# Projection inputs of blocks 1 to 3: normalised in place on ScalarE, turned in 32x32 blocks by VectorE

## The chip, the cores and the metric

The kernel runs on one core of a Trainium2 chip. The metric is the device time of one execution in microseconds; the number given for a kernel is the median of several runs. The engines named below are TensorE (PE, with its weight loads PEld), VectorE (DVE), ScalarE (ACT), GpSimd (POOL) and SyncE (SP, which only issues transfers here). Each works through its own queue of instructions in order, and semaphores hold an instruction until what it needs is there.

## What is computed

```python
xn = layernorm(x)                       # x: 2048 x 512, mean and variance over the 512
q, k, v = split(xn @ wqkv)              # 32 heads of 16
s = softmax(q k^T / 4) v  @ wo          # full attention over 2048 keys
f = (silu(xn @ w_gate) * (xn @ w_up)) @ w_down      # 512 -> 1792 -> 512
out = x + s * silu(f)
```

All inputs and the output are float32. Only the step from `x` to the transposed, normalised `xn` that the projections read is touched by the change.

## The kernel before

The 2048 rows are cut into four blocks of 512 rows, and each block into four tiles of 128 rows. The kernel has two stages. The first, some 148 us, makes the projections: for each block in turn, twelve output tiles, eight of them for features of q and k (`feature_tile`) and four for values (`value_tile`). In block 0 the value tiles come first (slots n = 0 to 3) and the feature tiles after them (n = 4 to 11); in blocks 1 to 3 the feature tiles are n = 0 to 7 and the value tiles n = 8 to 11. The second stage, all the rest of the time, is the attention, with the feed-forward network woven into it (`run`, `fill`, `ffn`).

An output tile (`project`, L648) is twelve matmuls on one PSUM bank. Operands are split into a rounded part and the rest (`hi`, `lo`), so for each of the four 128-wide chunks c of the inner dimension there are three matmuls in this order: hi with the weights' hi, lo with the weights' hi, hi with the weights' lo. Four PSUM banks (`pps`) take turns. After a feature tile ScalarE squares it (L701) and rounds it into `parts` (L702), VectorE subtracts to get the rest (L703), and SyncE stores both. After a value tile ScalarE copies it into `vt` (L719).

The projections need the normalised rows with features on the partitions, as `xt[b % 2]`, a pair of tiles hi and lo; two pairs take turns by block. While block b is projected, block b+1 is made ready in pieces between its slots, and the order is written out by hand in the loop at L745 to L827; each engine runs its share in that program order:

- `load_x` (L546): four transfers of 128 rows into `xin`, which is the tile `facc` (shown as such in the profile). Issued at n = 2 of block 0 and n = 1 of blocks 1 and 2.
- `stats` (L608) on VectorE for one tile at each of n = 2 to 5, and `rates` (L613) at n = 5: a chain of small VectorE operations around one square root on ScalarE (L616), which gives `rs`, one over the standard deviation.
- `norm` (L625) on VectorE for one tile at each of n = 6 to 9: (x - mean) * rs, into `xn`.
- `turn_x` (L641) at n = 8, 9 and twice at n = 10: four TensorE transposes of 128x128 into a bank of `acc` (L631), then ScalarE rounds it into hi (L636) and VectorE subtracts into lo (L639). After the last tile GpSimd's queue issues the two stores of the pair to `xt_d` (L645), from where the feed-forward network reads it hundreds of microseconds later.

Other work on the same queues in this stage: `split_w` (L568) rounds a tile of weights on ScalarE (L574) and subtracts on GpSimd (L575). In block 0 it is called at slot n for the weights of the tile n + 2, up to n = 9. `copy_fx` (L727, L732) puts one of sixteen pieces of block 0's `xt` into `fx` on ScalarE; it is called after the tile in each slot from n = 3 of block 0 to n = 6 of block 1. `flush` (L740) sums the squares of the tiles made so far with small matmuls (L663, in `squares`) and takes their peak; it stands at n = 0 of block 1 for block 0, and behind tile n = 8 in blocks 1 to 3. The sums need ScalarE's squares of all the eight feature tiles.

## Time and profile before

| | us |
|---|---|
| median of 3 runs | 1405.37 (1405.2 to 1405.68) |
| the profiled execution | 1405.18 |
| its span in the trace | 1403.4 |
| block 0 to 3 of the projections start at about | 6, 46, 83, 119 |
| PE busy over the span | 1395.8 |
| ACT busy over the span | 1082.7 |
| DVE busy over the span | 753.5 |
| POOL busy over the span | 90.6 |

A timeline row gives the start, the length, the engine, the line of the kernel, the operation, what it writes and reads, how many instructions are merged in the row, and in brackets the idle time before it with what ended it. The length of an instruction is from its start to its end; the next one on the same engine often starts somewhat before that end, so the cost of a row in a queue is the distance between starts. On TensorE this is marked: the lengths of matmuls overlap, and only the distance from start to start tells what one costs.

### The profile page before, as it was taken

The numbers are of one execution on the slowest core, as the hardware profiler recorded it, in microseconds if no ns is written. First come the engines' busy times: TensorE is split into PE (matmuls) and PEld (weight loads), VectorE is DVE, ScalarE is ACT, GpSimd is POOL, SyncE is SP. The second block draws the span as 40 slices with busy tenths as digits, with TensorE's granted clock in tenths as the row PEclk, the third lists the DMA queues.
The fourth block names the chain that finished last, engine by engine and source line by source line (L and its number), as shares of the span: only waits on it lengthen the run. The fifth ranks groups of instructions, "written<-read, shape, count | busy, mean of one in ns | idle before, by whom it ended". The sixth has DMA issues, their size and how long they took to land.

```text
span 1403.4 us, 27734 instructions
## 1 busy us (share of the span) xinstructions
PE 1395.8 (99%) x11227; PEld 847.1 (60%) x11227; DVE 753.5 (54%) x1291; ACT 1082.7 (77%) x1235; POOL 90.6 (6%) x104
## 2 busy tenths in 40 slices
PE   9999999999999999999999999999999999999998
PEld 7777756556555655565556556655655565565554
DVE  5544455345645553555456645654565446556655
ACT  6733587778788877887887788778877887888885
POOL 4200200000000000000000000000000000000333
PEclk9999999999999999999999999999999999999999
DMA  6768651033544521144524303256224113224333
GB/s 219 263 248 247 181 128 43 13 103 88 122 102 103 125 50 35 47 118 107 131 64 104 101 13 73 73 143 145 65 73 109 37 46 73 66 89 162 102 99 113
DMA packets 126956, 148.17 MB, mean 106 GB/s; under 512 B 12524, under 2 KB 79340, under 8 KB 126052
## 3 DMA queue, kind: packets, MB, share of 16 engines
q1 hardware_dynamic: 121620, 125.79, 34.2%
q0 software_dynamic: 4912, 20.12, 3.9%
q8 instruction: 91, 1.49, 0.4%
q14 instruction: 45, 0.37, 0.1%
q10 hardware_dynamic: 288, 0.39, 0.1%
HBM read 106.68 MB, written 39.58 MB: 104 GB/s over the span
## 4 chain that ended last, share of the span: by engine, by line
PE 88%; ACT 0%; DVE 0%; issue 0%; DVEq 0%; ACTq 0%
PE acc L406 32%; PE bankx L186 24%; PE score L888 17%; PE banky L186 12%; PE acc L888 3%; PE acc L1015 0%; PE banky L1015 0%; ACT pr L961 0%; ACT pr L894 0%; PE score L1015 0%; DVE y L1022 0%; DVE fx L280 0%; DVE part L300 0%; DVE y L191 0%; DVE pr L947 0%
## 5 line engine op out<-in xcount | busy, mean ns | idle before, releaser
L894 ACT ACTIVATE pr<-score 128x1024 f32<-128x1024 f32 x856 | 810.6, 1032 | 229.3 <-PE score L888 227.8
L406 PE MATMUL acc<-pr,vst 128*17 128x512 f32 x4096 | 461.9, 593 | 0.0
L888 PE MATMUL score<-qst,kst 50*128 50x512 f32 x1712 | 392.0, 413 | 0.0
L186 PE MATMUL bankx<-fx,guh 64*128 64x512 f32 x896 | 333.4, 393 | 0.1
L186 PE MATMUL banky<-fx,guh 64*128 64x512 f32 x896 | 324.5, 392 | 0.0
L406 PEld LDWEIGHTS acc<-pr,vst 128*17 128x17 f32 x4096 | 108.8, 97 | 286.4 <-issue 262.6
L888 PEld LDWEIGHTS score<-qst,kst 50*128 50x128 f32 x1712 | 176.0, 184 | 147.7 <-issue 67.2
L947 DVE COPY pr<-acc 128x512 f32<-128x512 f32 x168 | 116.2, 691 | 192.5 <-PE acc L888 187.0
L186 PE MATMUL bankx<-wd,hh 64*128 64x512 f32 x672 | 200.2, 392 | 0.0
L186 PE MATMUL banky<-wd,hh 64*128 64x512 f32 x672 | 197.8, 393 | 0.0
L186 PEld LDWEIGHTS bankx<-fx,guh 64*128 64x128 f32 x896 | 166.4, 186 | 18.0 <-issue 0.9
L186 PE MATMUL bankx<-fx,gul 64*128 64x512 f32 x448 | 175.4, 391 | 0.0
L186 PE MATMUL banky<-fx,gul 64*128 64x512 f32 x448 | 175.4, 391 | 0.0
L961 ACT ACTIVATE pr<-pr 128x1024 f32<-128x1024 f32 x168 | 172.5, 1079 | 0.0
L186 PEld LDWEIGHTS banky<-fx,guh 64*128 64x128 f32 x896 | 166.3, 186 | 6.1
L953 DVE COPY pr<-acc 128x512 f32<-128x512 f32 x168 | 116.2, 692 | 73.8 <-PE acc L888 60.3
L888 PE MATMUL acc<-qst,kst 50*128 50x512 f32 x336 | 135.4, 403 | 0.1
L239 DVE SCALAR_TENSOR_TENSOR ga<-th,bankx 128x512 f32<-128x512 f32 x56 | 38.5, 688 | 178.2 <-ACT th L238 178.2
L186 PEld LDWEIGHTS bankx<-wd,hh 64*128 64x128 f32 x672 | 124.9, 186 | 12.4
L186 PEld LDWEIGHTS banky<-wd,hh 64*128 64x128 f32 x672 | 124.4, 186 | 3.6
L186 PEld LDWEIGHTS bankx<-fx,gul 64*128 64x128 f32 x448 | 83.7, 187 | 10.3
L186 PEld LDWEIGHTS banky<-fx,gul 64*128 64x128 f32 x448 | 83.5, 186 | 3.6
(168 smaller groups left out, 1308.7 us busy)
## 6 DMA issues: line engine op xcount, KB each, us to landing
gur<-in_B_w_gate_dram SPq DMA_DIRECT2D x56, 256.0 KB
gur<-in_B_w_up_dram SPq DMA_DIRECT2D x56, 256.0 KB
wdr<-in_B_w_down_dram SPq DMA_DIRECT2D x56, 256.0 KB
kst<-k_d SPq DMA_DIRECT2D x192, 64.0 KB
qst<-q_d SPq DMA_DIRECT2D x192, 64.0 KB
fx<-xt_d SPq DMA_DIRECT2D x24, 512.0 KB
q_d<-parts SPq DMA_DIRECT2D x16, 512.0 KB
k_d<-parts SPq DMA_DIRECT2D x16, 512.0 KB
```

Of the source, the lines that this page charges most:

```text
L186: mm(banks[i], lhs[halves[i]], rhs[halves[i]], start=start, stop=stop)
L239: dve.scalar_tensor_tensor(ga, th, 1.0, bankx, op0=ALU.add, op1=ALU.mult)
L406: mm(acc[0][h * 32:h * 32 + DH + 1], v[:, kt % CT, h * (DH + 1):(h + 1) * (DH + 1)], probs[kt, h // 2][:, h % 2], start=kt == 0, stop=kt = ...
L888: mm(bank, k[r, j, kc * P:(kc + 1) * P], qst[u % 2][r, j], start=True, stop=True)
L894: act(pr, score[slot], AF.Exp, scale=0.25)
L947: dve.tensor_copy(probs[kt, j][:, 0], spare_bank)
L953: dve.tensor_copy(probs[kt, j][:, 1], spare_bank)
L961: act(probs[kt, j], probs[kt, j], AF.Exp, scale=0.25)
```

## The change

For blocks 1 to 3 the rows are normalised in place by ScalarE: `norms` first makes `off = -mean * rs` for the four tiles in one small VectorE operation and then runs four activations `xin * rs + off` with both as per-partition columns. They stand where `rates` stands, at n = 5 of block 0 and, since the statistics move one slot earlier, at n = 4 of blocks 1 and 2; there `load_x` moves from n = 1 to n = 0 as well. VectorE's `norm` goes.

The transposes on TensorE go, too. VectorE turns the rows in 32x32 blocks: `turn_quarter` takes 32 partitions of `xin` (quadrant g) and writes the blocks of one feature quarter to 32 partitions (quadrant q) of a new tile `xw`, sixteen instructions for a block of rows, each of 512 elements on 32 partitions. They stand ahead of the tile of a slot: in block 0 at n = 6 to 11 in numbers of 2, 3, 3, 2, 3, 3, in blocks 1 and 2 at n = 5 to 11 in numbers of 2, 2, 2, 3, 2, 2, 3. The rounding into hi and the subtraction into lo, which were done by row tiles at n = 8 to 10, are done by chunks c in `split_block` behind the tile and the other work of n = 11, and the two stores to `xt_d` behind them. Block 0 keeps the old way.

```diff
+TURNS = [[(max(0, min(16, s * (n - f) // d)), max(0, min(16, s * (n + 1 - f) // d))) for n in range(12)]
+         for f, s, d in ((6, 8, 3), (5, 16, 7))]
...
+        xw = pc.tile([P, DT, TB], F32, name="xw")
...
+        off = pc.tile([P, NT], F32, name="off")
...
             split_x(b, t, turn(t), between)
-            if t == NT - 1 and b:
-                for j in range(2):
-                    pool.dma_start(xt_d[b, j], xt[b % 2][j].bitcast(F32))
+
+        def norms():
+            dve.scalar_tensor_tensor(off, mv[:, :, 0], -1.0, rs, op0=ALU.mult, op1=ALU.mult)
+            for t in range(NT):
+                act(xin[:, t], xin[:, t], AF.Identity, scale=rs[:, t:t + 1], bias=off[:, t:t + 1])
+
+        quarter = [slice(i * 32, (i + 1) * 32) for i in range(4)]
+
+        def turn_quarter(i):
+            q, g = divmod(i, 4)
+            dve.transpose(xw[quarter[q]].rearrange("p c (t g l) -> p g t c l", g=4, l=32)[:, g],
+                          xin[quarter[g]].rearrange("p t (c q d) -> p q t c d", q=4, d=32)[:, q])
+
+        def split_block(b):
+            hi, lo = xt[b % 2]
+            for c in range(DT):
+                nc.scalar.copy(hi[:, c], xw[:, c])
+                dve.tensor_sub(lo[:, c], xw[:, c], hi[:, c].bitcast(F32))
+            for j in range(2):
+                pool.dma_start(xt_d[b, j], xt[b % 2][j].bitcast(F32))
...
-                if n == (1 if b else 2) and more:
+                if n == (0 if b else 2) and more:
                     load_x(b + 1)
+                if more:
+                    for part in range(*TURNS[b > 0][n]):
+                        turn_quarter(part)
...
                 if more:
-                    if 2 <= n < 6:
-                        stats(n - 2)
-                    if n == 5:
+                    ahead = n - (1 if b else 2)
+                    if 0 <= ahead < NT:
+                        stats(ahead)
+                    if ahead == NT - 1:
                         rates(0, NT)
-                    if 6 <= n < 10:
-                        norm(n - 6)
-                    if 8 <= n < 11:
-                        turn_x(b + 1, n - 8)
-                    if n == 10:
-                        turn_x(b + 1, NT - 1)
+                        norms()
+                    if n == 11:
+                        split_block(b + 1)
```

## The prediction

> **What bounds the kernel now.** I read the page first, then the busy time by stage, then the timelines of the four engines in the projections.

> ```profile
> span 1403.4 us, 27734 instructions
> ...
> PE 88%; ACT 0%; DVE 0%; issue 0%; DVEq 0%; ACTq 0%
> ```

> The chain that ended last is TensorE's. So a microsecond taken from TensorE's queue, or added as a stall in it, moves the end by about as much. The next view has the stretches of block 0 behind its value tiles and of block 1, with the columns length, PE, PEld, DVE, ACT, POOL, granted clock, DMA share, GB/s.

> ```profile
> 22.00:46.00 24.00, 23.69 (x110) 19.09 (x110) 13.04 (x30) 21.42 (x34) 9.19 (x8) 1.00 0.63 216
> 46.00:83.00 37.00, 37.00 (x178) 28.98 (x177) 18.67 (x41) 21.64 (x34) 5.76 (x8) 1.00 0.61 224
> ```

> TensorE never rests; but in block 0 ScalarE is busy for 21.42 of 24 us, with no room for more, whereas in block 1 it has. That is the fact on which I build. The timeline of TensorE:

> ```profile
> 35.59 0.60 PE L631 MATMUL acc<-ident,xn 128*128 128x128 f32 x4
> 35.94 0.71 PE L656 MATMUL ps<-xt,wh 128*128 128x512 f32 x2
> ...
> 46.24 0.65 PE L656 MATMUL ps<-xt,wh 128*128 128x512 f32 x2
> ...
> 72.18 0.60 PE L631 MATMUL acc<-ident,xn 128*128 128x128 f32 x4
> 72.71 0.40 PE L663 MATMUL bankx<-sq,ind 128*32 128x512 bf16 x4
> ...
> 79.38 1.04 PE L631 MATMUL acc<-ident,xn 128*128 128x128 f32 x8
> 80.17 0.71 PE L658 MATMUL ps<-vh,xt 128*128 128x512 f32 x2
> ...
> 83.03 0.62 PE L656 MATMUL ps<-xt,wh 128*128 128x512 f32 x2
> 83.48 0.40 PE L656 MATMUL ps<-xt,wl 128*128 128x512 f32 x1
> 83.72 0.63 PE L656 MATMUL ps<-xt,wh 128*128 128x512 f32 x2
> ```

> **What goes.** Four transposes hold TensorE for 35.94 - 35.59 = 0.35 us. In block 1 the three places cost 0.53 (72.18 to 72.71), 0.35 and 0.79 (79.38 to 80.17): 1.67 us. Block 2 has the same three places; block 0 is taken below by its end. Three matmuls take 83.72 - 83.03 = 0.69, so 0.23 each and 2.8 us a tile. The norms and subtractions that leave VectorE, and the casts that leave slots 8 to 10 of ScalarE, lay beside TensorE.

> **What comes, block 0.** ScalarE's queue around the square root of the rates, VectorE's chain behind it, and GpSimd's subtraction of weights:

> ```profile
> 30.24 0.20 ACT L616 ACTIVATE nw<-ve 128x4 f32<-128x4 f32 x1 [0.71 <-DVE ve L615]
> 30.35 0.60 ACT L574 CAST wh<-wraw 128x512 fp32r<-128x512 f32 x1
> 30.86 0.59 ACT L701 ACTIVATE sq<-ps 128x512 bf16<-128x512 f32 x1
> 31.35 0.58 ACT L702 CAST parts<-ps 128x512 fp32r<-128x512 f32 x1
> 31.95 1.05 ACT L732 CAST fx<-xt 64x1024 fp32r<-64x1024 f32 x1
> 33.02 0.62 ACT L574 CAST wh<-wraw 128x512 fp32r<-128x512 f32 x1
> 33.55 0.59 ACT L701 ACTIVATE sq<-ps 128x512 bf16<-128x512 f32 x1
> ```

> ```profile
> 31.54 0.81 DVE L621 TENSOR_SCALAR nw<-nw 128x4 f32<-128x4 f32 x1
> 32.38 0.58 DVE L623 TENSOR_SCALAR rs<-nw,rs 128x1 f32<-128x1 f32 x4
> ...
> 68.14 0.17 DVE L621 TENSOR_SCALAR nw<-nw 128x4 f32<-128x4 f32 x1
> 68.35 0.58 DVE L623 TENSOR_SCALAR rs<-nw,rs 128x1 f32<-128x1 f32 x4
> ```

> ```profile
> 31.03 1.29 POOL L575 TENSOR_TENSOR wl<-wraw,wh 128x512 fp32r<-128x512 f32 x1 [2.54 <-ACT wh L574]
> ```

> Today ScalarE takes the square root at 30.24 and goes on. Changed, the next instructions in its queue are the four norms, and they need the end of the rates: 32.38 + 0.58 = 32.96, less 0.64, since L621's 0.81 lies beside the GpSimd pass at 31.03, which is now later, and takes 0.17 in block 1; plus the new `off`, some 0.2 like its small neighbours. So ScalarE stands until 32.55. Behind it wait, on the same engine, the weights of tile 8, the square and cast of tile 6, and everything after.

> A norm (128x512, SBUF to SBUF, two per-partition columns) has no row. From below: 0.51, the step from the weight cast at 30.35 to 30.86. From above I set 0.80. I take 0.62, the same cast with no overlap (33.02). Four: 2.5 us, to 35.05.

> A turn (512 elements on 32 partitions) has no row either. The nearest:

> ```profile
> L442 DVE STREAM_TRANSPOSE o<-on x15: 700/703/714, 356.1 to 1355.6; 128x512 f32<-128x512 f32 x15
> ```

> ```profile
> 1393.01 0.45 DVE L1038 STREAM_TRANSPOSE y<-on 128x256 f32<-128x256 f32 x1
> 1393.38 0.41 DVE L417 STREAM_TRANSPOSE o<-acc 128x256 f32<-128x256 f32 x1
> ```

> `copy_fx` above, 1.05 us for 1024 elements on 64 partitions, says that fewer partitions don't make a pass shorter. Two transposes in a row overlap by 0.08, so 0.62 from below; 0.90 from above, for the strided blocks. I take 0.73, no overlap.

> The ScalarE queue from 35.05: a slot (weights, square, cast, `copy_fx`) takes 33.55 - 30.86 = 2.69, without weights 2.16. Squares start: tile 6 at 35.55, 7 at 38.25, 8 at 40.95, 9 at 43.65, 10 at 45.8, 11 at 47.95; its `copy_fx` ends at 50.1. VectorE in step: turns of n = 6 to 36.55, subtraction of 6 to 37.3, three turns 39.5, subtraction 40.1, three turns 42.3, subtraction 42.9, two turns 44.4, subtraction (cast ready 44.75) 45.35, three turns 47.55, subtraction 48.15, three turns 50.35. Both arrive together. TensorE first stands at tile 8: its low weights need ScalarE (35.65), then GpSimd's 1.29: 36.95, where today tile 8 runs at 35.59 less 2.8, 32.8. After that each tile finds its weights just in time, and tile 11 ends at about 47.7. Then the hi of chunk 0: 50.4 to 51.0; VectorE's last `parts` to 50.95, lo of chunk 0 to 51.75. The second matmul of block 1 runs at 51.8; today at 46.24 + 0.23 = 46.47. **Block 0: +5.3**, the lost transposes already in it.

> Later chunks don't wait: 0.61 (80.68 below, two in 1.29) per lo against 0.69 of TensorE.

> **Blocks 1 and 2.**

> ```profile
> 63.98 0.60 ACT L701 ACTIVATE sq<-ps 128x512 bf16<-128x512 f32 x1 [0.65 <-PE ps L656]
> 64.48 0.58 ACT L702 CAST parts<-ps 128x512 fp32r<-128x512 f32 x1
> 65.08 1.05 ACT L732 CAST fx<-xt 64x1024 fp32r<-64x1024 f32 x1
> ...
> 83.22 0.59 ACT L719 COPY vt<-ps 128x512 f32<-128x512 f32 x1 [2.09 <-PE ps L658]
> ```

> ```profile
> 80.68 1.29 DVE L639 TENSOR_TENSOR xt<-acc,xt 128x512 fp32r<-128x512 f32 x2 [2.52 <-ACT xt L636]
> ```

> At their ends ScalarE must first copy tile 11 (83.22), then hi of chunk 0: 83.70 to 84.30, lo to 85.05, where today the second matmul runs at 83.26: **+1.8 each**, no TensorE work being left to cover it. Inside block 1 the rates end 68.35 + 0.58 - 63.98 = 4.95 behind the square of their slot; with `off` and the norms of 2.5 that is 7.65, and the square of tile 7 comes two slots of 2.15 later and ends 0.6 after: 12.5 behind the square of tile 4. The sums at 72.71 stand about four tiles (11.2) behind that square, their last one at 11.4: a stall of **1.1**. Block 2 has no `copy_fx`; there the square ends at 10.5, no stall. Of PSUM, four banks give three tiles (8.4 us) of lag, against 5 needed.

> Moved transfers: the four x loads of blocks 2 and 3 go out one slot earlier on SP, behind one store fewer; statistics follow one slot earlier, as far behind as now. I cost both at nothing: VectorE has about 2 us idle per slot there; a load later than that would hold its queue, and the subtractions in it, by the excess. The two `xt_d` stores leave GpSimd's queue after the end of the block; nothing else queues there but memsets and a value store.

> **Sum.** Block 0 +5.3; block 1 -1.67 + 1.1 + 1.8 = +1.2; block 2 -1.67 + 1.8 = +0.1: **+6.6** on the profiled execution's 1405.18, 1411.8. It stands 0.2 under the median, so 1412.0. With 0.51 and 0.62 instead of 0.62 and 0.73 block 0's queue ends 0.45 to 0.7 earlier and block 1 gains 0.4: +5.5. With 0.80 for the norms +8; with 0.90 for the turns VectorE becomes the bound in block 0: sixteen times 0.17 is 2.7 there, and half as much in blocks 1 and 2, together +11.5.

> [...]

> **Rivals.**
> 1. The turns cost 0.85 or more: VectorE is the bound, +10 to +13, about 1416.5. [...]
> 2. Transfers are late in block 3.

> ```profile
> 115.00:119.00 4.00, 4.00 (x23) 3.38 (x22) 1.29 (x2) 1.56 (x3) 1.08 (x2) 1.00 0.14 59
> 119.00:148.00 29.00, 29.00 (x132) 22.51 (x131) 9.90 (x17) 9.78 (x19) 0.91 (x1) 1.00 0.96 293
> ```

> The stores of block 3's pair now fall wholly into a stretch with a DMA share of 0.96, and 86% of 4 us before it stays unused: up to 3.4 more, 1415.4.
> 3. TensorE's clock falls after its waits, of 2.7 and 3.2 us in block 0: a tile at half speed, +2.8, 1414.8. The granted clock here is 1.00 throughout, but no idle stretch as long occurs. [...]
> 4. The lag of ScalarE is absorbed: tile 11 of block 0 would end at 44, its square, cast and `copy_fx` take 2.4, hi and lo 1.5, so +1.2 there, and no stall at the sums: +1.4, 1406.8. Against it stands 21.42 of 24.
> 5. Faster: the splits of hi and lo stay hidden at all three ends, and only the transposes count, 1.67 three times: -5.0, 1400.2. It decides if the three waits together stay under 5.0, which needs the casts ahead of tile 11's evacuation on ScalarE; the program order puts them behind.

> **Chances.** Forecast (+4.5 to +9) 0.72; rival 1 0.09, rivals 2 and 3 together 0.08, rival 4 0.06, rival 5 0.05. What a measurement tells from no change is 0.2%, 2.8 us: slower 0.88, same 0.07, faster 0.05. The range leaves out rivals 4 and 5 and the upper half of rival 1: 1409.0 to 1416.5.

> **What would show it.** Right: no L631 behind block 0; TensorE idle near 33 to 36 us for weights, and 48 to 51 us for the cast of chunk 0, about 2 at the two later ends; ScalarE idle before the norms by 2 us, released by VectorE; norms at 0.6 to 0.7, turns at 0.7. Wrong: norms or turns far from these rows, ScalarE not standing before the norms, or an idle stretch of TensorE in block 3.

## The result and the profile after

The changed kernel takes 1424.26 us (median of 4 runs, 1423.36 to 1426.16) against 1405.53 before: 1.0135 times as long, 95% interval 1.0118 to 1.0153, some 18.7 us more. The profiled execution took 1423.36 us. The forecast was 1412.0, and its range ended at 1416.5: the direction was right and the size was not. Its page begins:

```profile
span 1421.6 us, 27684 instructions
...
PE 1400.8 (99%) x11179; PEld 845.2 (59%) x11179; DVE 781.3 (55%) x1330; ACT 1091.7 (77%) x1247; POOL 90.1 (6%) x104
```

TensorE still counts as busy 99%. The waits are a small part of the span, so they have to be read in the timeline of the projections. First TensorE's, with the idle time before a row and its releaser in brackets:

```profile
36.14 1.19 PE L677 MATMUL ps<-xt,wh 128*128 128x512 f32 x2 [3.10 <-ACT wh L576]
37.50 0.79 PE L677 MATMUL ps<-xt,wl 128*128 128x512 f32 x1 [0.17 <-POOL wl L577]
...
52.17 0.50 PE L677 MATMUL ps<-xt,wh 128*128 128x512 f32 x1 [2.75 <-ACT xt L663]
52.89 0.50 PE L677 MATMUL ps<-xt,wh 128*128 128x512 f32 x1 [0.23 <-DVE xt L664]
...
57.75 0.73 PE L677 MATMUL ps<-xt,wh 128*128 128x512 f32 x2
...
82.18 0.38 PE L684 MATMUL banky<-sq,ind 128*32 128x512 bf16 x1 [1.31 <-ACT sq L722]
...
93.02 0.50 PE L677 MATMUL ps<-xt,wh 128*128 128x512 f32 x1 [1.90 <-ACT xt L663]
93.75 0.51 PE L677 MATMUL ps<-xt,wh 128*128 128x512 f32 x1 [0.22 <-DVE xt L664]
...
97.97 0.63 PE L677 MATMUL ps<-xt,wh 128*128 128x512 f32 x2
...
133.19 1.52 PE L677 MATMUL ps<-xt,wh 128*128 128x512 f32 x2 [3.54 <-ACT xt L663]
...
138.70 0.63 PE L677 MATMUL ps<-xt,wh 128*128 128x512 f32 x2
...
164.84 0.49 PE L188 MATMUL bankx<-fx,guh 64*128 64x512 f32 x1
```

All five waits of the forecast are there: the weights of tile 8 at 36, the three block starts at 52, 93 and 133, the sums of squares at 82. Their places in the kernel before, for the comparison (the start of tile 1 in blocks 1 and 2, the start of block 3, and the first matmul of the feed-forward network):

```profile
49.68 0.73 PE L656 MATMUL ps<-xt,wh 128*128 128x512 f32 x2
...
85.82 0.63 PE L656 MATMUL ps<-xt,wh 128*128 128x512 f32 x2
...
119.06 0.62 PE L656 MATMUL ps<-xt,wh 128*128 128x512 f32 x2
...
147.99 0.49 PE L186 MATMUL bankx<-fx,guh 64*128 64x512 f32 x1
```

At the end of the projections the changed kernel is 164.84 - 147.99 = 16.85 us late, of 18.2 in the span. Stage by stage, from second matmul of a block to second matmul of the next, with the block's first tile taken apart:

| stretch | lost, us | forecast |
|---|---|---|
| to the second matmul of block 1 (52.89, before 46.47) | 6.4 | 5.3 |
| first tile of block 1, to 57.75 (before 49.68) | 1.65 | 0 |
| rest of block 1, to 93.75 (before 83.26) | 2.4 | 1.2 |
| first tile of block 2, to 97.97 (before 85.82) | 1.65 | 0 |
| rest of block 2, to the second matmul of block 3 (about 133.9, before 119.29) | 2.45 | 0.1 |
| first tile of block 3, to 138.70 (before 121.85) | 2.25 | 0 |

The three first tiles, 5.55 us, were not in the sum at all. There the granted clock (behind the counts of PE in this view of TensorE alone: length, busy, granted clock, DMA share, GB/s) is halved:

```profile
52.90:53.20 0.30, 0.30 (x1) 1.00 1.07 416
53.20:53.50 0.30, 0.30 (x2) 0.62 1.06 396
...
56.20:56.50 0.30, 0.30 (x2) 0.50 1.08 266
56.50:56.80 0.30, 0.30 (x2) 0.69 0.77 280
56.80:57.10 0.30, 0.30 (x2) 1.00 1.06 362
```

It falls at 53.3, in the middle of the work and not in the wait, and comes back at 56.7. In 3.4 us at 0.50 TensorE does half of the work, so it loses 1.7: the 1.65 of the table. It does the same from 94.2 to 97.6, from 131.8, still in the wait, to 138.6, and behind the first wait, from 36.2 to 39.6.

The other excess is VectorE's. Its timeline, and ScalarE's casts into hi:

```profile
32.45 0.16 DVE L649 SCALAR_TENSOR_TENSOR off<-mv,rs 128x4 f32<-128x4 f32 x1
35.61 1.41 DVE L657 STREAM_TRANSPOSE xw<-facc 32x512 f32<-32x512 f32 x2 [3.00 <-ACT facc L651]
...
48.77 2.14 DVE L657 STREAM_TRANSPOSE xw<-facc 32x512 f32<-32x512 f32 x3
...
117.52 1.41 DVE L657 STREAM_TRANSPOSE xw<-facc 32x512 f32<-32x512 f32 x2 [3.00 <-ACT facc L651]
...
127.48 5.01 DVE L657 STREAM_TRANSPOSE xw<-facc 32x512 f32<-32x512 f32 x7
```

```profile
32.65 2.93 ACT L651 ACTIVATE facc<-facc,off,rs 128x512 f32<-128x512 f32 x4 [2.11 <-DMA q_d<-parts]
35.49 0.60 ACT L576 CAST wh<-wraw 128x512 fp32r<-128x512 f32 x1
...
50.55 1.04 ACT L753 CAST fx<-xt 64x1024 fp32r<-64x1024 f32 x1
51.50 2.17 ACT L663 CAST xt<-xw 128x512 fp32r<-128x512 f32 x4
...
92.35 2.18 ACT L663 CAST xt<-xw 128x512 fp32r<-128x512 f32 x4 [0.61 <-DVE xw L657]
...
132.52 2.18 ACT L663 CAST xt<-xw 128x512 fp32r<-128x512 f32 x4 [2.25 <-DVE xw L657]
```

The bracket of the norms in block 0 names a transfer, but they start 0.04 us behind the end of `off` on VectorE (32.45 + 0.16): ScalarE stands for VectorE there, as forecast. In block 2 VectorE stands for 3.00 us until the norms are made, and from 117.5 it is never idle until the last turn ends at 132.5: sixteen turns, three subtractions and two reductions. Tile 11 ends at 129.5. The cast waits 2.25 us for VectorE there, and 0.61 in block 1; in block 0 it doesn't wait for it: the cast follows the last `copy_fx` at once, so ScalarE's own queue arrives last.

### The profile page after: what moved, and what is told of

The parts are those of the page before. It is cut to its first block, busy times and chain, and to the rows that moved or that the text cites. A ratio compares the mean times of both kernels' runs of the same rounds, so it can differ in the third digit from the quotient of the medians.

```text
span 1421.6 us, 27684 instructions
## 1 busy us (share of the span) xinstructions
PE 1400.8 (99%) x11179; PEld 845.2 (59%) x11179; DVE 781.3 (55%) x1330; ACT 1091.7 (77%) x1247; POOL 90.1 (6%) x104
## 4 chain that ended last, share of the span: by engine, by line
PE 86%; ACT 0%; DVE 0%; issue 0%; DVEq 0%; ACTq 0%
PE acc L408 31%; PE bankx L188 23%; PE score L910 17%; PE banky L188 12%; PE acc L910 3%; PE acc L1037 0%; ACT pr L916 0%; PE banky L1037 0%; ACT pr L983 0%; PE score L1037 0%; DVE pr L969 0%; DVE y L1044 0%; DVE fx L282 0%; DVE y L193 0%; DVE part L302 0%
## 5 line engine op out<-in xcount | busy, mean ns | idle before, releaser
L677 PE MATMUL ps<-xt,wh 128*128 128x512 f32 x256 | 86.8, 420 | 11.7 <-ACT xt L663 8.2
```

Of the source, the lines that this page charges most:

```text
L677: mm(ps, w, a[:, c], start=n == 0, stop=n == 3 * DT - 1)
```

## The experiments

My theory from these rows: the loss is waits of TensorE at the ends of the blocks, held by ScalarE's queue and by VectorE's turns at once in block 0 and by VectorE alone in blocks 1 and 2, plus a halved clock that the waits bring on. Its rivals: that the clock comes at no cost; that ScalarE's norms are the cause; that the order at the block's end alone is.

**Keeping TensorE busy in its waits.** In the changed kernel:

```diff
+        def warm(b, n):
+            hi = xt[b % 2][0]
+            for i in range(n):
+                mm(acc[0], wh[:, 0, i % DT], hi[:, i % DT], start=True, stop=True)
...
+                if b and n == 0:
+                    warm(b - 1, (0, 10, 8, 14)[b])
+                if b == 0 and n == 8:
+                    warm(0, 12)
                 made = make(b, i)
```

> The changed kernel with idle matmuls (128x512, into the unused bank acc[0], 0.233 us each) put into TensorE's queue where it waits: 12 ahead of tile 8 of block 0, and 10, 8 and 14 ahead of the first tile of blocks 1, 2 and 3. Theory (waits plus a halved clock behind them): the waits for ScalarE and VectorE stay where they are, the granted clock stays at 1.00, and the slow first tiles (+1.65, +1.66, +2.24 us) and about 0.6 us at the end of block 0 go: about 6 us less than the changed kernel, 1418. Rival (waits alone make the loss, the clock comes with them at no cost): no change, 1424.

Measured: 1417.47 us, 1.0090 [1.0073, 1.0107] of before. TensorE:

```profile
48.39 2.50 PE L769 MATMUL acc<-xt,wh 128*128 128x512 f32 x10
51.64 0.49 PE L677 MATMUL ps<-xt,wh 128*128 128x512 f32 x1 [0.74 <-ACT xt L663]
52.36 0.50 PE L677 MATMUL ps<-xt,wh 128*128 128x512 f32 x1 [0.23 <-DVE xt L664]
...
55.67 0.72 PE L677 MATMUL ps<-xt,wh 128*128 128x512 f32 x2
```

The casts for block 1 come half a microsecond earlier than in the changed kernel, as the slow tile 8 is gone; from the second matmul to tile 1 it takes 3.31 us instead of 4.86, and the mean granted clock of the execution is 1.000 (0.994 in the changed kernel). Work that computes nothing saves 6.8 us in the median; 5.8 of them lie in the projections, whose end comes at 159.06 instead of 164.84. So the halved clock costs about 6 us, and the other 12 are the waits themselves, less the transposes saved. The rival falls.

**Norms on VectorE instead of ScalarE.**

```diff
-            dve.scalar_tensor_tensor(off, mv[:, :, 0], -1.0, rs, op0=ALU.mult, op1=ALU.mult)
             for t in range(NT):
-                act(xin[:, t], xin[:, t], AF.Identity, scale=rs[:, t:t + 1], bias=off[:, t:t + 1])
+                dve.tensor_scalar(xin[:, t], xin[:, t], mv[:, t, 0:1], rs[:, t:t + 1], op0=ALU.subtract, op1=ALU.mult)
```

> The changed kernel with the four norms done in place by VectorE (as tensor_scalar with mean and rs) instead of ScalarE. Theory (VectorE's sixteen turns fill its queue to the end of each block, so ScalarE's stand is not what bounds the ends of the blocks): the stall at tile 8 of block 0 and the stall at the sums of squares in block 1 (1.3 us) go, the turns start 1 us earlier, the three waits at the ends of the blocks shrink by about 1 us each and stay: 1420 (1418 to 1422). Rival (ScalarE's norms are the main cause, as the prediction had it for block 0): the wait at the end of block 0 goes with them, 6.4 + 1.3 us: 1416 or less.

Measured: 1418.03 us (1416.02 to 1418.6), 1.0089 [1.0072, 1.0106]. The start of block 1 on TensorE and the cast for it on ScalarE:

```profile
52.05 1.52 PE L675 MATMUL ps<-xt,wh 128*128 128x512 f32 x2 [7.50 <-ACT xt L661]
```

```profile
51.38 2.18 ACT L661 CAST xt<-xw 128x512 fp32r<-128x512 f32 x4 [4.65 <-DVE xw L655]
```

No wait at tile 8 or at the sums any more; tile 11 of block 0 ends five microseconds sooner; and block 1 starts at 52.05, where it started before at 52.17. ScalarE is free and waits 4.65 us for VectorE's turns. So the norms on ScalarE made waits inside the blocks, but did not alone set the place at which block 0 ends. The rival falls. The three waits did not each shrink by 1 us, though: they are 7.50, 2.20 and 2.27 us, where they were 2.75, 1.90 and 3.54. The clock came out otherwise, too, with a mean of 0.995 over the execution: behind the long wait the matmuls step 0.43 us apart instead of 0.23, until 58.3, and behind the third 0.23, which is worth 2.2 of the 4.4 us by which these projections end sooner.

**The same, and each turn on half of its elements.**

```diff
-            ..."p c (t g l) -> p g t c l", g=4, l=32)[:, g],
-            ..."p t (c q d) -> p q t c d", q=4, d=32)[:, q])
+            ..."p c (t g l) -> p g t c l", g=4, l=32)[:, g, :2],
+            ..."p t (c q d) -> p q t c d", q=4, d=32)[:, q, :2])
```

> The changed kernel with the norms on VectorE, and with each turn on half of its elements (256 instead of 512 on 32 partitions; the other half of xw is zero, so the output is not the reference's). Theory (with the norms off ScalarE, VectorE's turns alone hold the end of block 0): 16 x 0.3 us less VectorE time, so the wait there falls from 7.5 us to about 3.5, and what is left is ScalarE's evacuation of tile 11 with the first cast; in blocks 1 and 2 about 1.8 us each are left: 1410 (1408.5 to 1412). Rival (the order at the ends of the blocks alone, the cast standing behind tile 11, makes the waits, whatever VectorE does): within 2 us of the kernel with the norms on VectorE, 1416 or more.

Measured: 1410.04 us, 1.0035 [1.0022, 1.0049]. The three block starts:

```profile
47.62 1.52 PE L676 MATMUL ps<-xt,wh 128*128 128x512 f32 x2 [3.18 <-ACT xt L662]
...
87.01 0.50 PE L676 MATMUL ps<-xt,wh 128*128 128x512 f32 x1 [1.32 <-ACT xt L662]
...
123.28 0.50 PE L676 MATMUL ps<-xt,wh 128*128 128x512 f32 x1 [1.19 <-ACT xt L662]
```

As expected: 7.50 becomes 3.18. What is left in blocks 1 and 2, 1.2 to 1.3 with 0.23 for the first lo, is the price of the order alone: the casts standing behind tile 11's evacuation, that is, behind ScalarE's reading of it out of PSUM. In block 0 `copy_fx` stands there too. Behind the wait of 3.18 the matmuls also step 0.43 us apart instead of 0.23, from 47.6 to 53.6, which costs about 3 us. The three waits, 6.2 us, and the clock together are more than the transposes saved, and so the kernel is slower than before even with VectorE's turns half as long.

**Half turns with the norms on ScalarE.** The same two lines of the diff on the changed kernel.

> The changed kernel, norms on ScalarE as it has them, with each turn on half of its elements (output not the reference's). Theory (in block 0 ScalarE's queue and VectorE's arrive within 0.6 us of each other, so taking VectorE's time away alone leaves the wait there; in blocks 1 and 2 VectorE alone was late, by 0.6 and 2.25 us): first tile of block 1 within 0.6 us of the changed kernel's, blocks 1 and 2 some 0.6 and 2.3 us less, the clock part of block 3 less: 1420 (1418.5 to 1421.5). Rival (VectorE is the bound in all three blocks): the wait of block 0 shrinks by 4 us too, 1415 or less.

Measured: 1416.84 us, 1.0085 [1.0069, 1.0100], below the range I gave.

```profile
53.42 0.50 PE L678 MATMUL ps<-xt,wh 128*128 128x512 f32 x1 [2.75 <-ACT xt L664]
...
92.17 0.50 PE L678 MATMUL ps<-xt,wh 128*128 128x512 f32 x1 [1.32 <-ACT xt L664]
...
129.91 0.49 PE L678 MATMUL ps<-xt,wh 128*128 128x512 f32 x1 [1.19 <-ACT xt L664]
```

The waits are as the theory has them: 2.75 in block 0 unchanged, 1.90 and 3.54 down to 1.32 and 1.19. So in block 0 either queue alone suffices for the delay, and in blocks 1 and 2 it was VectorE. The times are not as I said. Stretches of this run (the granted clock behind the counts of POOL, as in the views of the kernel before):

```profile
36.00:40.00 4.00, 3.51 (x7) 2.32 (x8) 2.01 (x5) 3.93 (x8) 2.21 (x2) 0.50 0.28 106
40.00:50.00 10.00, 10.00 (x40) 8.06 (x39) 6.50 (x13) 8.55 (x12) 6.25 (x7) 0.89 0.46 167
50.00:54.00 4.00, 1.17 (x4) 0.38 (x2) 2.35 (x5) 3.34 (x7) 0.38 (x1) 1.00 0.52 193
54.00:58.00 4.00, 3.86 (x21) 2.60 (x22) 1.89 (x4) 1.92 (x5) 1.11 (x2) 1.00 1.01 297
...
90.00:94.00 4.00, 2.46 (x8) 1.42 (x7) 1.85 (x4) 2.77 (x5) 0.94 (x2) 0.92 0.89 322
94.00:98.00 4.00, 4.00 (x13) 3.21 (x12) 0.64 (x2) 0.69 (x2) 1.04 (x2) 0.66 1.02 376
...
128.00:132.00 4.00, 2.57 (x11) 1.56 (x10) 2.11 (x4) 2.66 (x5) 1.20 (x2) 1.00 0.52 195
132.00:136.00 4.00, 4.00 (x19) 3.25 (x18) 1.08 (x2) 1.07 (x2) 0.78 (x2) 1.00 1.01 372
```

Block 1 starts 1.25 us later than in the changed kernel, not within 0.6, mainly since the clock was halved behind the wait for tile 8 until 42.1 instead of 39.6. It then stayed at 1.00 behind the wait at 53 us, which has the same length as the one that halved it in the changed kernel, and behind the one at 130; but it fell at 93.3, behind a wait of only 1.32. All told the projections end 5.5 us sooner (159.34 instead of 164.84). The medians are 7.4 apart, so some 2 us of the low total lie elsewhere, and no row accounts for them.

**What the transposes are worth.** In the kernel before, the 48 transposes left out:

```diff
         def turn_x(b, t, between=None):
-            split_x(b, t, turn(t), between)
+            av = acc[t % 2].rearrange("p (c f) -> p c f", f=P) if b else turn(t)
+            split_x(b, t, av, between)
```

> The kernel before with the 48 transposes of blocks 1 to 3 on TensorE left out (the casts read what lies in the banks, so the output is not the reference's). It gives what the transposes are worth, the most the change could win. Theory (1.67 us a block in blocks 1 and 2, 2.0 in block 0): 5.0 to 5.4 us less than before, 1400.3. Rival (they lie beside other work): under 1 us, 1405.

Measured: 1401.73 us, 0.9978 [0.9969, 0.9988]: 3.5 us, not 5. The rest is seen at the start of block 1:

```profile
45.73 0.50 PE L657 MATMUL ps<-xt,wh 128*128 128x512 f32 x1 [1.28 <-ACT xt L636]
```

With nothing between tile 10 and tile 11 ScalarE's last cast in block 0 comes 1.3 us late, and the subtraction behind it another 0.33. The transposes had covered that.

**Pauses of a known length in the kernel before.** Ahead of four tiles a small matmul waits for extra passes of ScalarE.

```diff
+            if pause[0]:
+                for _ in range(pause[0]):
+                    nc.scalar.copy(gap, xh[:, 0].bitcast(F32))
+                mm(ps[:, :P], gap[:, :P], gap[:, :P], start=True, stop=True)
             n = 0
```

> The kernel before with four pauses of TensorE, made by one small matmul that waits for 1, 1, 3 and 4 extra passes of ScalarE: ahead of tiles 0 and 5 of block 2 and of tiles 0 and 5 of block 3. TensorE should be idle for about 1.3, 1.9, 2.3 and 3.4 us, 8.9 in all. Theory (the clock is halved for 3.4 us after a stretch of 3.4 us on a fixed grid in which TensorE was busy for about 40% or less): the short ones cost only themselves, one or two of the long ones 1.7 us more; 1405.5 + 8.9 + 1.7 to 3.4 = 1416 to 1418, and the granted clock shows 0.50 behind the pauses whose stretch was mostly idle. Rival (only an idle time as long as a whole stretch of 3.4 us halves the clock): 1414.4 and 1.00 throughout.

Measured: 1418.60 us, 1.0097 [1.0080, 1.0113]: 13.4 more than before, and 0.6 above the range I gave. The idle times sum to 9.1.

```profile
84.31 0.49 PE L655 MATMUL ps<-gap 128*128 128x128 f32 x2 [1.32 <-ACT gap L654]
```

```profile
100.43 0.49 PE L655 MATMUL ps<-gap 128*128 128x128 f32 x2 [1.68 <-ACT gap L654]
```

```profile
125.42 0.80 PE L655 MATMUL ps<-gap 128*128 128x128 f32 x2 [2.49 <-ACT gap L654]
```

```profile
144.91 0.49 PE L655 MATMUL ps<-gap 128*128 128x128 f32 x2 [3.63 <-ACT gap L654]
```

```profile
123.00:125.40 2.40, 0.00 (x0) 0.93 0.98 396
125.40:128.60 3.20, 3.18 (x9) 0.52 0.99 367
```

After 1.32 and 1.68 us the clock stays at 1.00; after 2.49 and 3.63 it is halved for about 3.4 us. That is 9.1 of idle time, some 3.4 for two halved stretches, and about 1 for the four small matmuls. A pause shorter than 3.4 us, that of 2.49, is enough; the rival falls.

**A version without the waits.** Block 1 as before; blocks 2 and 3 turned by VectorE with the norms on VectorE, three slots earlier, and split ahead of tile 11:

```diff
+                if b == 0 and n == 2:
+                    load_x(1)
+                if b < 2 and n == 11:
+                    load_x(b + 2)
...
+                elif more:
+                    if n < 2:
+                        stats(2 * n)
+                        stats(2 * n + 1)
+                    if n == 1:
+                        rates(0, NT)
+                        norms()
+                    if n == 10:
+                        split_block(b + 1)
```

> A version that takes from the change what the runs so far leave: block 1 as in the kernel before (norms on VectorE, transposes on TensorE); blocks 2 and 3 with the norms in place on VectorE, x loaded at n = 11 of the block before, statistics at n = 0 and 1, two turns in each slot from n = 2 to 9, and the split behind tile n = 10, so that tile 11 covers it. Theory (VectorE has room in blocks 1 and 2 if it starts three slots earlier, and a split ahead of tile 11's evacuation waits for nothing): no wait at the starts of blocks 2 and 3, the clock at 1.00, and 1.67 us of transposes saved in each: 3.3 us less than before, 1402. Rival (x comes too late, or VectorE is full again): waits of 1 us and more at the two starts, 1405 or more.

Measured: 1402.41 us (1401.57 to 1404.12), 0.9981 [0.9972, 0.9990] of the kernel before. No wait at the starts of blocks 2 and 3; one is left in the middle of block 1:

```profile
65.36 0.73 PE L679 MATMUL ps<-xt,wh 128*128 128x512 f32 x2 [1.28 <-DVE parts L726]
```

A tile waits 1.28 us for a PSUM bank that VectorE has not read yet, with statistics, rates and norms ahead in its queue by the program's order. The rival is in part right here: VectorE is late, though inside block 1 and not at the two starts. Norms and turns spread out:

```diff
-                        norms()
+                    if 2 <= n < 4:
+                        norms(2 * n - 4, 2 * n - 2)
```

> The version above with VectorE's work of blocks 1 and 2 spread: norms two at a time at n = 2 and 3 instead of all at n = 1, turns in numbers of 2, 3, 3, 2, 3, 3 from n = 4 to 9. Theory (the one wait left in block 1 there, 1.28 us at 65 us for a PSUM bank, came from a subtraction queued behind statistics, rates and norms on VectorE at once): that wait goes, no other comes: 1401.1. Rival (VectorE is then late at the split of n = 10): a wait at the starts of blocks 2 and 3 in its place, 1402.4 or more.

Measured: 1401.89 us (1401.20 to 1402.83), 0.9973 [0.9963, 0.9984]. That wait is gone, and TensorE waits nowhere between block 1's start and the end of the projections. The intervals of the two versions overlap, so only the vanished wait is shown, not a difference in time between them. Both beat the kernel before, by 2.7 and 3.6 us, and the changed one. They start earlier and split earlier at once, so the runs don't say what each of the two is worth.

## Why the prediction was wrong

**What held.** That TensorE's queue is the bound and ScalarE full in block 0; that a norm and a turn cost about what was taken. The four norms step by (35.49 - 32.65) / 4 = 0.71, between the 0.62 taken and the upper bound, 0.80. Seven turns take 5.01, 0.72 each against 0.70 for one, so turns in a row don't overlap; 0.73 was taken. ScalarE took up the norms at 32.65 (32.55 forecast), the last turn of block 0 ended at 50.9 (50.35), the sums stalled 1.31 (1.1). The end of block 0 was forecast at 51.8 and came at 52.89; about half a microsecond of the difference is tile 8 at the halved clock, since it went away with the idle matmuls.

**What failed first: the clock, rival 3.** The forecast gave it 2.8 us, as an alternative, with less than 0.08 of chance. The clock was halved four times, and that cost about 6 us by the run that kept TensorE busy: a term of the sum, not an alternative. Two errors are in that. No row supports so small a chance: the longest idle time of TensorE in the trace of before is 1.38 us, so that trace could not say what the clock does behind 2.7 or 3.2; the runs showed it halved behind the waits of 3.10 and 2.75 of the changed kernel and behind a pause of 2.49, and not behind the wait of 2.75 of the run with half turns. And the waits were taken singly: in the changed kernel the 3.41 us before the fall at 94.2 hold the wait of 1.90, the first matmul, and the next wait of 0.22 us.

**What failed second: the sentence "VectorE has about 2 us idle per slot there".** It was written for the moved transfers, and it stood for all of VectorE in blocks 1 and 2, whose queue I walked in block 0 only. From the rows of the prediction: the norms end 7.65 behind the square of tile 4, then come sixteen turns of 0.73, three subtractions and two reductions of about 0.7, 15.2, so the last turn ends at 22.8. Tile 11 of block 2 ends seven tiles of 2.8 and 0.55 for the sums (72.71 to 73.26 in the kernel before) behind that square, at about 20.1, and its copy 0.6 later. The 2 us of lateness could have been had from the same rows; measured are 2.25 in block 2, and in block 1, where the sums hold TensorE 1.3 longer, 0.61. The terms +1.8 for the two block ends lacked that lateness. What they priced, the order of copy and cast, was right: in the run with half turns on the changed kernel, block 2 takes 37.75 us from second matmul to second matmul against 36.03 before; less 1.66 for the halved clock and plus the 1.67 of transposes that it saved, that is 1.7.

**What the range lacked.** The uncertain rows, norms and turns, set its width, and both came out near their values. Of the 12 us missing in the forecast about 6 came from a mechanism left out of the sum and some 3 from a queue not walked in blocks 1 and 2. The other rivals fell: a turn costs 0.72 at most, TensorE has no wait inside block 3, and all five waits came.

**What stays open.** Of the 18.2 us in the span 1.35 arise behind the projections. There the other kernels here take 1255.3 to 1256.5 us, the kernel before 1255.4 and the changed one 1256.8; no row accounts for it; that it is variation between executions is possible and not shown.

## What to carry to other kernels

Work taken off a full TensorE pays only if what replaces it is finished before the queue gets there: here the transposes held TensorE for some 5 us in sum, of which leaving them out won 3.5, and casts standing behind the evacuation of the last tile left it idle for 1.4 to 3.2 us a block even with the turns halved. Walk every queue that receives work through every block, not only the one that looks fullest. And where a change makes the bounding engine wait at all, price the clock behind the wait, here about 6 us of the 18.7, with the wait.

## What the runs showed of the hardware

In the stretch before the fall at 94.2 TensorE had been idle for 2.1 us of 3.4. A pause of 2.49 us halved the clock and one of 1.68 did not; two waits of 2.75 us, one in the changed kernel and one in that with half turns, differed in it. On the raster that each run's other falls give, 2.3 us of the first lie in one stretch, and the second is cut into 1.7 and 1.05. So a share of a raster stretch that is idle, with the phase, is a likely reading. It is not shown, and one limit doesn't fit all: in the run with half turns the clock fell at 93.3 though TensorE had been idle for only 1.5 us of that stretch, less than the 1.7 that did not halve it at 52.4. The four executions of the changed kernel have mean granted clocks from 0.991 to 0.994, the slowest the lowest, as it would be if the phase differed between executions.
